# A hand-planned attention and MLP kernel: weight loads that either SyncE or ScalarE may issue, and larger planned costs for SyncE's transfers

## The chip, the cores and the metric

One core of one Trainium2 chip runs the kernel. The metric is the device time of one execution in microseconds, the median of several runs. Matmuls run on TensorE (PE), elementwise work on VectorE (DVE) and ScalarE (ACT), memsets on GpSimd (POOL). Transfers are issued by SyncE (SP) or ScalarE and carried out by 16 DMA engines which all issuers share.

## The reference

Attention in which a query sees only the keys of its own hash bucket, then a two-layer MLP on its output. In numpy, cut to what matters:

```python
# q, k, v: (4, 8, 768, 64) fp32; proj: (64, 6); w_in: (512, 2048); w_out: (2048, 512)
q_bucket = sum(((q @ proj) > 0) * 2**arange(6)); k_bucket likewise
scores = where(q_bucket == k_bucket, q @ k.T / 8, -1e9)
attn = softmax(scores)
x = (attn @ v), heads side by side            # (3072, 512)
h = x @ w_in
g = where(h > 0, h, exp(min(h, 0)) - 1)
out = g @ w_out                               # (3072, 512)
```

## The kernel before

**Numbers.** The values have the precision of fp32, but the matmuls are fast ones on f16: a number is split into a high f16 part and the rest, and three products (high-high, high-rest, rest-high) are summed. So nearly every operand has a "hi" and a "lo" operation.

**Tiles and stages.** The 4 batches are cut in half along the queries: 8 chunks of 384 queries. In each chunk 4 pairs of heads make 32 pairs, n = 0 to 31; each pair has 6 score tiles of 128 queries by 768 keys, 192 in all. A tile goes: scores on PE (L946), maximum on DVE (L969), exponential with sum on ACT (L997), normalised hi (L358) and lo (L363) into a buffer hl, transposed by a DMA of SP into PT (L1053), and the average with v on PE (L1130). PT has two slots of three tiles each. The first four pairs have no hi and lo: PE turns their probabilities (flip, L1013) and the turned tiles are moved out of PSUM into PT by ACT or DVE.

Queries and keys of a pair are loaded by SP, scaled and split, and transposed by a DMA of SP (K at L731, Q at L771; pair 0 on PE). The sign bits come from a small matmul z (L805), a test on DVE (L826, into zb) and small copies of SP (L835) into the transposed operand, two to four for each Q or K. For chunk 0 the loads of its four pairs come first of all.

**Weights.** The 32 slices of w_in and w_out (512 KB each) come in as raw 64-bit words by SP (L464). Every fourth goes to one area of its own ("raw", one slot), the others into U, which has three slots. ACT then takes the top half of each word (L480), DVE joins it with the low one into W (L483) and with that frees the slot; PE squares and sums the slice for a bound on its size (acc, L494). When all of w_in or w_out has been bounded, the slices are split into hi and lo. The MLP of a chunk follows on PE as 16 blocks of F (h, L1192), with E, R, M, H, L on ACT and DVE (L1216 to L363), and of S (o, L1244), interleaved with the scores of the next chunk.

**What sets the order.** Each operation is registered by `add` (L72) with the engines that may run it, its reckoned duration (`took`), a due place, its dependences and ring buffers. `order` (L104) is a list scheduler: again and again it takes the operation that can begin earliest on any engine (the smallest due place decides among those that can begin at once), and its sequence becomes the program order of each engine's queue. An engine other than the first of its list takes an operation only if the first is busy more than YIELD longer (0.9 us before 240 us, 2.5 us after). For SP a transfer lands at `dma + 1000 + slow`: `dma` is a running end of the transfers (each adds its `late`), and `slow` delays the landing alone. A bulk load (weights, v) isn't issued before `dma - BACKLOG` (4.5 us), and at most 8 transfers of SP are under way. The loads of the weights follow each other in order of their number. Where PE would idle in the first 32 us the list puts in dummy matmuls ("spin", L1337).

Durations and landings are only the plan's: on the chip every queue runs its instructions in the planned order, and each waits for its semaphores.

Of the kernel before, what the change touches and what calls it, by code (L numbers as in the profile page):

```python
# [34 lines left out]
NEAR = {"P": 0.0, "V": 0.0, "A": 0.0, "S": 0.0, "G": 0.0}  # L35
BACKLOG = 4500.0
VD = -40
YIELD = (900.0, 2500.0)
FULL = 240e3
STRICT = ("v",)  # L40
# [14 lines left out]

class Op:

    __slots__ = ("engs", "eng", "run", "took", "late", "due", "deps", "after", "new", "left", "next", "start", "free", "end", "slow", "bulk", "cols", "name")

    def __init__(self, **kw):  # L60
        self.start = None
# [5 lines left out]
class Plan:  # L67
# [4 lines left out]
    def add(self, engs, run, took, due, deps=(), after=(), new=(), use=(), late=0.0, slow=0.0, bulk=False, cols=128, name=""):  # L72
        o = Op(
            engs=engs, eng=None, run=run, took=dict(zip(engs, took if type(took) is tuple else (took,))), late=late, due=due, deps=[d for d in deps if d], after=[a for a in after if a],
            new=list(new), slow=slow, bulk=bulk, cols=cols, name=name,
        )
        for b in (*new, *use):
            b.users.append(o)
        self.ops.append(o)
        return o  # L80

    def seen(self, o, e):
        return o.free if o.eng == e and e != "S" else o.end

    def ready(self, o, e):
        t = o.start[e]
# [17 lines left out]
    def order(self):  # L104
        ops = self.ops
        for o in ops:
            o.left = len(o.deps) + len(o.after)
            for d in o.deps:
                d.next.append(o)
            for a in o.after:  # L110
                a.next.append(o)
        open_ = {e: [] for e in "PVAGS"}

        def opened(o):
            o.start = {e: max([0.0] + [self.seen(d, e) for d in o.deps] + [a.start for a in o.after]) for e in o.engs}
            for e in o.engs:
                open_[e].append(o)

        free = {e: 0.0 for e in open_}
        cols = 128  # L120
        dma = 0.0
        sent = []
        for o in ops:
            if o.left == 0:
                opened(o)
        done, spun = [], []
        while len(done) < len(ops):
            best = None
            for e, waiting in open_.items():
                at, some = None, []  # L130
                for o in waiting:
                    t = self.ready(o, e)
                    if t is None:
                        continue
                    t = max(t, free[e])
                    if e == "S" and o.bulk:
                        t = max(t, dma - BACKLOG)
                    if e != o.engs[0] and free[o.engs[0]] < t + YIELD[t > FULL]:
                        continue
                    some.append((t, o.due, o, e))  # L140
                if some:
                    near = min(x[0] for x in some) + NEAR[e]
                    at = min((x for x in some if x[0] <= near), key=lambda x: x[1::-1])
                if at is not None and (best is None or at[0] < best[0]):
                    best = at
            assert best is not None, [(e, [(o.name, o.due) for o in w][:6]) for e, w in open_.items()]
            t, _, o, e = best
            o.eng = e
            for x in o.engs:
                open_[x].remove(o)  # L150
            for b in o.new:
                b.slot = len(b.ring.made) % b.ring.cap
                b.ring.made.append(b)
            took = o.took[e]
            if e == "P":
                if self.spin is not None and t < SPIN[1]:
                    gap = t - max(free[e], SPIN[0]) - SPIN[2]
                    if gap > 0.0:
                        spun.append(self.spin(max(free[e], SPIN[0]), int(gap // 214.0) + 1))
                elif t < COLD:  # L160
                    took *= 1.8
                if o.cols != cols:
                    took += SWITCH
                    cols = o.cols
            if e == "S":
                if len(sent) >= 8:
                    t = max(t, sent[-8])
                dma = max(dma, t + 950.0) + o.late
                o.end = dma + 1000.0 + o.slow
                sent.append(o.end)  # L170
            else:
                o.end = t + took + o.late + SIGNAL[e]
            o.start = t
            o.free = free[e] = t + took
            o.left = None
            done.append(o)
            for x in o.next:
                x.left -= 1
                if x.left == 0:
                    opened(x)  # L180
        return sorted(spun + done, key=lambda o: o.start)
# [18 lines left out]
def lsh_attention_moe(  # L200
# [10 lines left out]
    nc = tc.nc  # L211
    B, H, S, D = q.shape
# [32 lines left out]
    add = plan.add  # L245
# [197 lines left out]
    def weight_ops():  # L443
# [4 lines left out]
        def one(i):  # L448
            o = int(i >= NSI)
# [9 lines left out]
                src = wo64[(i - NSI) * P : (i - NSI + 1) * P, :]  # L459
            due = i - 14.0 + 0.4 * o * (i - NSI)  # L460

            def load():
                t.t = area["raw" if raw else "U"][t.slot]
                nc.sync.dma_start(t.t["in"], src)  # L464

            l = add("S", load, 460.0, due - 6, after=([first_k["q"]] if i == 2 else []) + staged[-1:], new=[t], late=1600.0, slow=1000.0, bulk=True, name=f"w{i}load")
            staged.append(l)
            if not raw:
                in_u.append(i)
# [121 lines left out]
    def prep_ops(ns):  # L591
# [11 lines left out]
        for n, p in zip(ns, ps):  # L603
# [6 lines left out]
            def track(o):  # L610
                regs.append(o)
                return o
# [96 lines left out]
        for x, (n, p) in enumerate(zip(ns, ps)):  # L709
# [9 lines left out]
            if kw:  # L719
                nat, K = buf(f"natk{own}"), buf("K")  # L720
                kbuf[b, p] = K

                def k_hi(e, i=i, s=s, x=x):
                    times(s["natk"][:, :, :D], i["kf"], sc.t[:, x : x + 1], e)

                def k_lo(i=i, s=s, x=x):
                    left_over(s["natk"][:, :, D:], i["kf"], sc.t[:, x : x + 1], s["natk"][:, :, :D])

                def k_tr(K=K, s=s):
                    K.t = [okp.tile([P, 2 * NC, P], F16, tag=y, name=y, bufs=NP) for y in ("K1", "K2")]  # L730
                    nc.sync.dma_start_transpose(K.t[0], flat(s["natk"]))  # L731

                def k_dup(K=K):
                    nc.vector.tensor_copy(flat(K.t[1])[:D], flat(K.t[0])[:D])

                hi = track(add("AV", k_hi, either(2 * NC * D, pointer=True), due - 1, [chain], new=[nat], use=[sc, i["kb"]], name=f"k{n}hi"))
                lo = track(add("V", k_lo, vec(2 * NC * D, 1, True), due - 1, [hi], use=[sc, i["kb"], nat], name=f"k{n}lo"))
                if n == 0:

                    def k_new(K=K):  # L740
                        K.t = [okp.tile([P, 2 * NC, P], F16, tag=y, name=y, bufs=NP) for y in ("K1", "K2")]

                    tr = turned(s["natk"], k_new, lambda K=K: K.t[0], K, nat, [lo], due, f"k{n}tr")
                    first_k["tr"] = tr[-1]
                else:
                    tr = [track(add("S", k_tr, 1700.0, due, [lo], new=[K], use=[nat], late=2100.0, name=f"k{n}tr"))]
                dup = add("V", k_dup, vec(2 * NC * P, 4), due + 3, tr, use=[K], name=f"k{n}dup")
                cps = bits_ops(
                    f"k{n}", [(0, lambda u, K=K: flat(K.t[0])[:, u * HALF : (u + 1) * HALF]), (1, lambda u, K=K: flat(K.t[0])[:, u * HALF : (u + 1) * HALF])],
                    4, 0, lambda u, K=K: flat(K.t[1])[D : D + 2 * NB, u * HALF : (u + 1) * HALF], tr, [K], due + 3, 8, n < DIRECT,  # L750
                )
                kdone[b, p] = [*tr, dup, *cps]
# [23 lines left out]
            if n == 0:  # L776
                tr = turned(s["qq"], q_new, lambda O=O: O.both, O, nat1, [lo, dup], due + 1, f"q{n}tr", (nat2,))
            else:
                tr = [track(add("S", q_tr, 1700.0, due + 1, [lo, dup], new=[O], use=[nat1, nat2], late=2100.0, name=f"q{n}tr"))]
            i["tr"] = tr  # L780
            first_k.setdefault("q", tr[-1])
        both = [ns] if w == 2 else [[n] for n in ns]
# [14 lines left out]
    def bits_ops(name, ways, quads, which, target, deps, use, due, mms, direct):  # L797
# [34 lines left out]
        for u in range(quads):  # L832

            def copy(u=u):
                nc.sync.dma_start(target(u), zb.t[u * QD : u * QD + 2 * NB])  # L835

            cps.append(add("S", copy, 760.0, due, [s], use=[zb, *use], late=100.0, name=name + "cp"))
        return cps


# [76 lines left out]
    def pair_ops(n):  # L917
# [8 lines left out]
        for at in range(2 * HC):  # L926
# [112 lines left out]
            for y, (g, t_, PT_, pt_, _) in enumerate(duo):  # L1039
# [10 lines left out]
                def trp(t_=t_, PT_=PT_, hl=hl, make=make):  # L1050
                    if make:
# [7 lines left out]
                lows[g] = [h]  # L1059
                filled.append(  # L1060
                    add(
                        "S", trp, 1650.0, g + 2.0, [l], after=[] if make else PT_.users[:1], new=[PT_] if make else [],
                        use=[hl] + ([] if make else [PT_]), late=2100.0, name=f"tr{g}",
                    )
                )
        x16, av = buf("x16"), buf("av")
# [307 lines left out]
```

## Time and profile before

| | |
|---|---|
| median of 3 runs | 857.09 us (855.75 to 858.48) |
| profiled execution | 857.44 us |
| its span, first to last instruction | 855.7 us |
| PE busy | 815.4 us, 95% |
| ACT busy | 707.0 us, 83% |
| DVE busy | 678.9 us, 79% |
| SP's DMA queue, share of the 16 engines' span | 72.5% |

How to read it: a busy time counts instructions that compute, and not those that issue transfers or wait. PE's time is modelled at its ends, since matmuls overlap. In the page's slices each digit is one fortieth of the span (21.4 us) in tenths. The granted clock (PEclk) is TensorE's, as a share of 2.4 GHz; 0.50 is 1.2 GHz. In a timeline the bracket behind an instruction is the idle time of its engine before it, with what ended it.

### The profile page before, as it was taken

To read this page: it belongs to the slowest core of one execution; us is meant where nothing else is said; L and a number is where in the kernel's file an instruction comes from. 1 tells how busy PE (TensorE), PEld (TensorE's weight loads), DVE (VectorE), ACT (ScalarE), POOL (GpSimd) and SP (SyncE) were. 2 spreads that over 40 slices of the span, in tenths; PEclk is the share of its full clock that TensorE was granted. 3 is DMA by queue.
4 is the path that set the end of the run, shared out by engine and by line. 5 is a ranking of instruction groups with operands and counts; after the bars stand their busy time and mean duration, and the time that the engine had idled before them with its cause. 6 is when DMAs were issued, how large, how long until landed. Compare 5 with 4: busy or idle time off the path is not lost. (4 is left out here: it accounts for less than half of the span.)

```text
span 855.7 us, 14941 instructions
## 1 busy us (share of the span) xinstructions
PE 815.4 (95%) x5322; PEld 439.8 (51%) x5322; DVE 678.9 (79%) x1511; ACT 707.0 (83%) x1301; POOL 4.8 (1%) x24
## 2 busy tenths in 40 slices
PE   8897888998999999999999999999999999999997
PEld 3365544554554555555555555545455555555553
DVE  5868999999997877988988788889888777773232
ACT  7789999999987889988988789888888778783543
POOL 2000000000000000000000000000000000000000
PEclk9989999999999999999999999999999999999999
DMA  9769667897889589958888888958877768552101
GB/s 298 191 204 293 200 113 130 164 217 122 169 157 178 112 185 209 201 98 154 173 150 131 144 185 191 212 105 151 154 153 141 130 106 155 99 105 38 38 1 38
DMA packets 364330, 128.21 MB, mean 150 GB/s; under 512 B 339112, under 2 KB 357216, under 8 KB 364256
## 3 DMA queue, kind: packets, MB, share of 16 engines
q1 hardware_dynamic: 363952, 127.13, 72.5%
q8 instruction: 42, 0.69, 0.3%
q14 instruction: 32, 0.26, 0.1%
q10 hardware_dynamic: 304, 0.13, 0.1%
HBM read 35.65 MB, written 6.29 MB: 49 GB/s over the span
## 5 line engine op out<-in xcount | busy, mean ns | idle before, releaser
L1192 PE MATMUL h<-X,W 128*128 128x384 f16 x1536 | 312.0, 326 | 4.1 <-ACT U L1220 4.1
L1244 PE MATMUL o<-W,U 128*128 128x512 f16 x1152 | 307.0, 379 | 0.4 <-DVE U L363 0.4
L997 ACT ACTIVATE pt<-pt,nb,sg 128x768 f32<-128x768 f32 x192 | 195.8, 1021 | 41.2 <-DVE nb L986 41.0
L1192 PEld LDWEIGHTS <-W 128*128 128x128 f16 x1536 | 148.3, 97 | 141.8 <-issue 10.3
L969 DVE TENSOR_SCALAR_CACHE_REDUCE pt<-s 128x768 f32<-128x768 f32 x180 | 171.2, 951 | 16.3 <-PE s L946 15.5
L363 DVE SCALAR_TENSOR_TENSOR hl<-pt,r,hl 128x768 f16<-128x768 f32 x168 | 165.2, 1013 | 8.4 <-ACT hl L358 8.3
L1244 PEld LDWEIGHTS <-U 128*128 128x128 f16 x1152 | 110.3, 97 | 101.8 <-issue 2.8
L946 PE MATMUL s<-K,O 128*128 128x384 f16 x720 | 147.8, 327 | 9.8 <-DVE pt L969 9.2
L358 ACT ACTIVATE hl<-pt,r 128x768 f16<-128x768 f32 x168 | 148.8, 928 | 1.0 <-ACT U L358 0.5
L1223 DVE SCALAR_TENSOR_TENSOR U<-U 128x384 f32<-128x384 f32 x128 | 70.9, 554 | 51.2 <-ACT U L1220 50.8
L946 PEld LDWEIGHTS <-O 128*128 128x128 f16 (+1 forms) x768 | 72.9, 98 | 68.5 <-issue 23.3
L1216 ACT ACTIVATE U<-h,ch 128x384 f32<-128x384 f32 x128 | 73.0, 570 | 40.5 <-PE h L1192 39.4
L358 ACT ACTIVATE U<-U,sgg 128x384 f16<-128x384 f32 x128 | 78.1, 610 | 25.6 <-DVE U L1223 25.6
L363 DVE SCALAR_TENSOR_TENSOR U<-U,sgg 128x384 f16<-128x384 f32 x128 | 78.6, 614 | 22.3 <-ACT U L358 19.9
L1130 PE MATMUL av<-PT,vhl 128*64 128x384 f16 x1008 | 90.2, 327 | 6.3 <-DMA PT<-hl 6.3
L1130 PEld LDWEIGHTS <-vhl 128*64 128x64 f16 x1008 | 57.7, 110 | 37.8 <-issue 11.4
L1220 ACT ACTIVATE U<-h,ch 128x384 f32<-128x384 f32 x128 | 72.9, 570 | 0.0
L1035 DVE TENSOR_SCALAR r<-sm 128x2 f32<-128x2 f32 x84 | 13.9, 166 | 30.5 <-ACT pt L997 30.2
L997 ACT ACTIVATION_READ_ACCUMULATOR pt<-pt,nb,sg 128x1 f32 x192 | 36.9, 192 | 0.0
L1013 PE MATMUL flip<-W,pt 128*128 128x128 f32 x144 | 23.6, 287 | 2.4 <-ACT PT L358 1.6
L358 ACT ACTIVATE X<-av 128x384 f16<-128x384 f32 x28 | 13.5, 481 | 13.6 <-PE av L1130 13.4
L363 DVE SCALAR_TENSOR_TENSOR X<-av,X 128x384 f16<-128x384 f32 x28 | 15.5, 554 | 11.3 <-ACT X L358 11.3
(134 smaller groups left out, 581.3 us busy)
## 6 DMA issues: line engine op xcount, KB each, us to landing
U<-in_moe_w_in_dram SPq DMA_DIRECT2D x12, 512.0 KB
vf<-in_v_dram SPq DMA_DIRECT2D x16, 384.0 KB
U<-in_moe_w_out_dram SPq DMA_DIRECT2D x12, 512.0 KB
qst<-in_q_dram SPq DMA_DIRECT2D x30, 192.0 KB
kst<-in_k_dram SPq DMA_DIRECT2D x14, 384.0 KB
out_dram<-W SPq DMA_DIRECT2D x16, 256.0 KB
PT<-hl SPq DMA_TRANSPOSE x168
W<-in_moe_w_in_dram SPq DMA_DIRECT2D x4, 512.0 KB
```

Source lines behind the costliest of these rows:

```text
L358: nc.scalar.activation(o, x, AF.Copy, scale=s)
L363: nc.vector.scalar_tensor_tensor(o, x, s, hi, ALU.mult, ALU.subtract)
L946: nc.tensor.matmul(s.t[:, y, :HALF], O[x][:rows, j * HC + t, :], K[x][:rows, j * NC + y * HC : j * NC + (y + 1) * HC, :].rearrange("p a b ...
L969: nc.vector.tensor_scalar(pt.t.rearrange("p (n e) -> p n e", n=2), s.t[:, :, :HALF], CLAMP, None, ALU.max, ALU.max, accum_out=m.t[:, y : y ...
L997: nc.scalar.activation(pt_.t, pt_.t, AF.Exp, bias=nb.t[:, y : y + 1], scale=sg_of(n), accum_out=sm.t[:, z : z + 1])
L1013: nc.tensor.transpose(hb.t[:, c * P : (c + 1) * P], pt_.t[:, (y * HC + c) * P : (y * HC + c + 1) * P], eye)
L1130: nc.tensor.matmul(av.t[j * D : (j + 1) * D], vs["hl"][p].t[:, j, c, vx, :], PTs[j].t[:, :, px, c, :], start=y == 0, stop=y == 3 * NC - 1,)
L1192: nc.tensor.matmul(h.t, WH[:, g * KT + t, wx, fc * P : (fc + 1) * P], xbuf[NP * ci + t].t[:, xx, :], start=t == 0 and y == 0, stop=t == KT ...
L1216: nc.scalar.activation(e.t, h.t, AF.Exp, scale=c["ch"])
L1220: nc.scalar.activation(hp.t, h.t, AF.Relu, scale=c["ch"])
L1223: nc.vector.scalar_tensor_tensor(e.t, e.t, -1.0, hp.t, ALU.add, ALU.min)
L1244: nc.tensor.matmul(banks[t][:, :DO], g16.t[:, gx, t * P : (t + 1) * P], WH[:, NSI + 1 + f, wx, :], start=f == 0 and y == 0, stop=f == NF - ...
```

## The change

Weight loads may now be issued by ScalarE as well ("SA" in place of "S"; SyncE is still the first choice), with a reckoned 0.50 us on SyncE and 0.62 us on ScalarE, where 0.46 us stood. What the list does for a transfer (landing, backlog, at most 8 under way) now goes by the operation being a transfer (`dma`) and not by its engine. SyncE's other transfers are reckoned longer, and land later by `SLACK`:

| transfer | reckoned on SP before | after | landing later by |
|---|---|---|---|
| transpose of K | 1.70 us | 1.90 in chunk 0, else 1.80 | 1.0 us |
| transpose of Q | 1.70 us | 2.70 in chunk 0, else 2.30 | 1.0 us |
| copy of bits | 0.76 us | 0.82 us | 0.5 us |
| transpose of probabilities | 1.65 us | 1.78 us | 1.5 us |

```diff
+SLACK = (1500.0, 1000.0, 500.0)
...
-            new=list(new), slow=slow, bulk=bulk, cols=cols, name=name,
+            new=list(new), slow=slow, bulk=bulk, dma="S" in engs, cols=cols, name=name,
...
-        return o.free if o.eng == e and e != "S" else o.end
+        return o.free if o.eng == e and not o.dma else o.end
...
-                    if e == "S" and o.bulk:
+                    if o.bulk:
                         t = max(t, dma - BACKLOG)
...
-            if e == "S":
+            if o.dma:
                 if len(sent) >= 8:
...
-            def load():
+            def load(e="S"):
                 t.t = area["raw" if raw else "U"][t.slot]
-                nc.sync.dma_start(t.t["in"], src)
-
-            l = add("S", load, 460.0, due - 6, after=([first_k["q"]] if i == 2 else []) + staged[-1:], new=[t], late=1600.0, slow=1000.0, bulk=True, name=f"w{i}load")
+                (nc.scalar if e == "A" else nc.sync).dma_start(t.t["in"], src)
+
+            l = add("SA", load, (500.0, 620.0), due - 6, after=([first_k["q"]] if i == 2 else []) + staged[-1:], new=[t], late=1600.0, slow=1000.0, bulk=True, name=f"w{i}load")
...
-                    tr = [track(add("S", k_tr, 1700.0, due, [lo], new=[K], use=[nat], late=2100.0, name=f"k{n}tr"))]
+                    tr = [track(add("S", k_tr, 1900.0 if early else 1800.0, due, [lo], new=[K], use=[nat], late=2100.0, slow=SLACK[1], name=f"k{n}tr"))]
...
-                tr = [track(add("S", q_tr, 1700.0, due + 1, [lo, dup], new=[O], use=[nat1, nat2], late=2100.0, name=f"q{n}tr"))]
+                tr = [track(add("S", q_tr, 2700.0 if early else 2300.0, due + 1, [lo, dup], new=[O], use=[nat1, nat2], late=2100.0, slow=SLACK[1], name=f"q{n}tr"))]
...
-            cps.append(add("S", copy, 760.0, due, [s], use=[zb, *use], late=100.0, name=name + "cp"))
+            cps.append(add("S", copy, 820.0, due, [s], use=[zb, *use], late=100.0, slow=SLACK[2], name=name + "cp"))
...
-                        "S", trp, 1650.0, g + 2.0, [l], after=[] if make else PT_.users[:1], new=[PT_] if make else [],
-                        use=[hl] + ([] if make else [PT_]), late=2100.0, name=f"tr{g}",
+                        "S", trp, 1780.0, g + 2.0, [l], after=[] if make else PT_.users[:1], new=[PT_] if make else [],
+                        use=[hl] + ([] if make else [PT_]), late=2100.0, slow=SLACK[0], name=f"tr{g}",
```

## Rows read from the trace of the kernel before

**Rows 1.** The page: busy us, share and instructions; clock and DMA in 40 slices.
```profile
PE 815.4 (95%) x5322; PEld 439.8 (51%) x5322; DVE 678.9 (79%) x1511; ACT 707.0 (83%) x1301; POOL 4.8 (1%) x24
...
PEclk9989999999999999999999999999999999999999
DMA  9769667897889589958888888958877768552101
```
**Rows 2.** Busy time by stage: stretch, length, busy us (instructions) by engine, clock, DMA, GB/s.
```profile
0.00:100.00 100.00, 85.86 (x624) 48.65 (x624) 77.11 (x197) 82.29 (x169) 4.76 (x24) 0.97 0.84 248
100.00:240.00 140.00, 125.45 (x841) 67.58 (x833) 135.33 (x300) 137.14 (x252) 0.00 (x0) 1.00 0.79 152
240.00:780.00 540.00, 533.01 (x3491) 286.83 (x3488) 444.58 (x975) 454.19 (x822) 0.00 (x0) 1.00 0.79 149
```
**Rows 3.** The same view in steps of 4 us: PE, PEld, DVE, ACT, POOL, clock.
```profile
28.00:32.00 4.00, 3.78 (x30) 1.66 (x30) 3.86 (x12) 0.10 (x1) 0.00 (x0) 1.00 0.44 101
32.00:36.00 4.00, 3.84 (x26) 1.98 (x24) 3.93 (x12) 3.14 (x6) 0.00 (x0) 1.00 0.48 92
36.00:40.00 4.00, 2.17 (x20) 1.12 (x18) 2.00 (x5) 2.53 (x8) 0.00 (x0) 1.00 0.99 297
40.00:44.00 4.00, 2.42 (x18) 1.51 (x18) 2.73 (x5) 4.00 (x10) 0.00 (x0) 0.90 0.66 205
44.00:48.00 4.00, 2.76 (x14) 1.92 (x13) 2.58 (x7) 1.31 (x4) 0.00 (x0) 0.50 0.40 77
```
**Rows 4.** Timeline of SP's queue, 22 to 96 us: start, length, instructions.
```profile
22.35 0.53 SPq L464 DMA_DIRECT2D W<-in_moe_w_in_dram  x1
...
28.20 3.22 SPq L835 DMA_DIRECT2D K<-zb  x4
31.52 1.54 SPq L835 DMA_DIRECT2D O<-zb  x2
33.16 1.47 SPq L731 DMA_TRANSPOSE K<-natk  x1
34.68 1.82 SPq L464 DMA_DIRECT2D U<-in_moe_w_in_dram  x3
...
47.97 0.45 SPq L464 DMA_DIRECT2D W<-in_moe_w_in_dram  x1
...
95.09 0.37 SPq L464 DMA_DIRECT2D U<-in_moe_w_out_dram  x1
```
**Rows 5.** Timeline of DVE: the joins of the first three loads into U.
```profile
26.03 1.88 DVE L483 SCALAR_TENSOR_TENSOR W<-U,X 128x512 int32<-128x512 int32 x3
```
**Rows 6.** Timeline of ACT, 32 to 48 us: the instructions behind its longest gaps.
```profile
32.46 1.03 ACT L997 ACTIVATE pt<-pt,nb,sg 128x768 f32<-128x768 f32 x1 [4.36 <-DVE nb L986]
...
39.34 0.78 ACT L480 ACTIVATE X<-U 128x512 f16<-128x512 bf16 x1 [1.47 <-DMA U<-in_moe_w_in_dram]
...
47.01 0.49 ACT L358 ACTIVATE PT<-flip 128x384 f32<-128x384 f32 x1 [2.54 <-PE flip L1013]
```
**Rows 7.** Timeline of PE: the bound sum behind the late decode.
```profile
40.90 0.40 PE L494 MATMUL acc<-W 128*128 128x128 bf16 x4 [2.05 <-DVE W L483]
```
**Rows 8.** Line 401, the issues on ACT's queue: min/median/max ns, first and last start.
```profile
L401 ACTq DMA_DIRECT2D pf<-in_proj_dram x2: 559/586/612, 0.8 to 1.4; - x2
```
**Rows 9.** Line 1053, the transposes of probabilities, in the same form.
```profile
L1053 SPq DMA_TRANSPOSE PT<-hl x168: 1382/1688/3224, 116.4 to 770.6; - x168
```
**Rows 10.** Waits from 240 to 780 us: total us, times, longest.
```profile
PE av L1130 <- DMA PT<-hl: 5.3, 4, 1.7
...
PE z L805 <- DMA O<-natq: 1.0, 1, 1.0
```
**Rows 11.** Waits of SP's queue from 56 to 100 us, in the same form.
```profile
SPq L464 <- DVE W L483: 19.9, 14, 4.5
```

More of the change, by code (lines that the diff above doesn't have):

```diff
@@ L56 @@
 class Op:
-    __slots__ = ("engs", "eng", "run", "took", "late", "due", "deps", "after", "new", "left", "next", "start", "free", "end", "slow", "bulk", "cols", "name")
+    __slots__ = ("engs", "eng", "run", "took", "late", "due", "deps", "after", "new", "left", "next", "start", "free", "end", "slow", "bulk", "dma", "cols", "name")
     def __init__(self, **kw):
```

## The prediction

> **What bounds the kernel now.** I read the page's totals first, then the busy time by stage, then the one stretch where everything stands still, and last the waits of the long middle stage.
>
> The totals [rows 1] show PE busy for 815.4 of 855.7 us, so TensorE is the bound over the whole span, and nothing can win more than its 40 us of gaps plus what a lowered clock costs. The stages [rows 2] tell where these gaps are. From 240 to 780 us PE is busy 533.0 of 540 us: 7.0 us of gaps. From 100 to 240 us PE is busy 125.5 of 140, while ACT has 137.1 and DVE 135.3: there ACT and DVE are the bound. In the first 100 us nobody is: PE 85.9, DVE 77.1, ACT 82.3. This is the stage of the weight loads, and a microsecond won there passes on, since what follows is a stage of work that ACT and DVE must do in any case and then one that PE must do in any case. The tail after 780 us holds none of the edited operations.
>
> Inside the first stage the stretch from 28 to 48 us stands out [rows 3]. Between 36 and 40 us PE, DVE and ACT are all half idle together. The clock then falls: 0.90 for 40 to 44 us and 0.50 for 44 to 48 us, which is 1.2 GHz, the lower of the two levels, just after PE's gaps. And right before, from 28 to 36 us, the DMA engines are at 0.44 and 0.48 with about 100 GB/s, while a moment later they do 297 GB/s at 0.99. The transfers were not short of engines; they had not been issued. The queue of SP shows why [rows 4]: K's four bit copies at 28.20 take 3.22 us (0.80 each), then O's two, then a transpose at 33.16, and only at 34.68 come three weight loads into U. Their three slots had been free since the three joins of DVE that run from 26.03 for 1.88 us, so until 27.91 [rows 5]. These loads stood 6.8 us behind small copies. The chain goes on: ACT's first decode of them starts at 39.34 after waiting for that DMA (4.66 us after issue) [rows 6], and PE's next bound sum at 40.90 waits 2.05 us for the join behind that decode [rows 7].
>
> **The change part by part: the loads.** ScalarE may take a weight load when the list finds SP busy more than 0.9 us longer (2.5 us after 240 us, where no weight load is left). The loads that SP issues directly behind transposes or copies are the candidates: one at 22.35, three at 34.68, four from 47.97 to 52.76, two at 79.40 and 80.01, and the one at 95.09, 11 of 32 [rows 4] (the first, the last and two places between). Copies count 0.82 us in the list and one alone is no ground to move a load, a transpose or a run of them is. I expect 6 to 10 loads on ACT, and take 8.
>
> What it gives: the loads of 34.68 could be issued at about 28.0, where ACT has just begun 4.36 us of idleness, waiting for the scores' bias until 32.46 [rows 6]. With 4.66 us to landing their data is there by 33, so ACT's waits of 1.47 us at 39.34 and, as the clock has no reason to fall, 2.54 us at 47.01 (for flips at the lower clock) go [rows 6]; a few tenths of the same kind follow until 52 us. I put the sum at 4.9 us of ACT. What is late next there is the chain of scores, maximum and bias; it is not touched.
>
> What it costs: an issue on ACT is seen in the two small loads of proj, 0.559 and 0.612 us [rows 8], the only ones behind no other work; for a 512 KB load no row exists on ACT. 0 is the lower bound (in one of ACT's holes), 0.61 the upper one. I take 0.45, between them, nearer to the upper row, and let half of the 8 fall into holes: 4 x 0.45 = 1.8 us. Bounds: 0 to 8 x 0.61 = 4.9 us. SP gets the same instructions off its queue, which is worth nothing by itself: SP waits far longer than it issues. Net of the loads: -4.9 + 1.8 = -3.1 us. The far end is that the whole stretch of 36 to 48 us is repaired: PE's gaps of 1.83, 1.58 and 1.24 us and the clock's 0.10 x 4 + 0.50 x 4 = 2.4 us [rows 3], 7.1 us in all, with free issues.
>
> **The larger costs and later landings.** They execute nothing. They change the order: operations of PE, DVE and ACT that need a transpose or a copy are listed later by 1.5 us (probability transposes), 1.0 us (K and Q) and 0.5 us (bits), and SP's own list is spread wider. The new 1.78 for a probability transpose stands against a median of 1.688 us [rows 9], the old 1.65 was also close, so SP's pace hardly changes. The landing is the part that matters: between 240 and 780 us PE waits 5.3 us in four waits for those transposes (the weight loads' view of PE, PEld, counts the same gaps) and 1.0 us for a Q transpose [rows 10]. Together that is 6.3 of the 7.0 us of gaps. A later listing puts F and S blocks in front of the average, work that is there. A wait vanishes where it is under 1.5 us; four waits of 1.3 us mean are around that. But each later average also holds its PT slot longer (two slots), and the next transposes into it begin later, so part of a wait comes back. I take a third of the 7.0 us: -2.3 us. Bounds: -6.3 us, all of them gone, and +6.3 us, as many new ones of the same size.
>
> **Sum.** The profiled execution is 857.44 us, 855.7 of span and 1.7 around it; the median of the three runs, 857.09, is 0.35 below, which is nothing here. 857.44 - 3.1 - 2.3 = 852.0 us.
>
> **A rule against it.** The DMA engines at 0.44 between 28 and 36 us [rows 3] say that a load issued earlier would land earlier. The Trainium skill (DMA: Bandwidth & Descriptors, section "Issuing engines are not separate DMA queues") holds that issuing from several engines only saves the sequencer's time to initiate a transfer, all of them running on the same 16 engines. By that rule the change would be near nothing, the second rival below; the trace disagrees for this stretch, since what holds the loads is their place behind SP's other instructions, not the engines.
>
> **The rivals.**
> First, faster by far: every gap named is repaired, 857.4 - 7.1 - 6.3 = 844.0 us. For it speaks that both stretches have one plain cause each. Against it, that the orders of five engines shift together, and that from 60 us on loads are limited by free slots, not by SP. Chance 0.10.
>
> Second, no change: the loads come earlier, yet the stage up to 100 us ends when it did. From 56 to 100 us the loads wait for the joins of DVE, 14 times, 19.9 us [rows 11], so SP is not what holds most of them, and the engines have little room: with only the issue time saved, 8 x 0.37 us of an SP [rows 4] that waits anyway, and the waits for PT merely moved, it is 857.4 + 0 to 1.8 us, 857 to 859. Chance 0.25.
>
> Third, slower: a load listed on ACT is not ready when ACT reaches it. Loads wait on a slot which the join on DVE frees, 1.42 us each (19.9 / 14) [rows 11]. On SP nobody stands behind such a wait; on ACT the exponentials, decodes and evictions do, and PE's flips behind these. From 60 to 240 us ACT has nothing to give [rows 2]. Four such waits (5.7 us) undo the 3.1 us and add 2.6 us; six cost 8.5 us, which with no gain from the landings gives 857.4 - 3.1 + 8.5 = 862.8 us. It decides from the fourth on. For it speaks that the list's times and the chip's drift apart; against it, that the candidates stand in stretches where their slots had been free for microseconds (6.8 us for those at 34.68). Chance 0.17.
>
> That the change does not do what it says, no load on ACT at all because copies of 0.82 us never reach 0.9 us, belongs to the second rival in its time; transposes of 1.9 and 2.7 us make it unlikely.
>
> **How the numbers follow.** About 0.3% (2.6 us) is what a measurement of this kernel can tell from no change. The forecast, 852.0, has 0.48; its own range is 848 to 857 (the loads from -4.9 with free issues to 0 with 4.9 of issues, the landings from two thirds of 7.0, -4.6, to 0), and the larger part, 0.42, is below 854.5. With the first rival's 0.10: faster 0.52. Within 0.3%: the second rival's 0.25 and the forecast's upper part, 0.06: 0.31. Slower: 0.17. To leave out no more than 0.2 the range reaches from 845.0, a little above the first rival, to 861.0, short of the third rival's six waits.
>
> **What would show each step.** In the profile after: weight loads on ACT's queue, the first of them near 28 us; the share of the DMA engines in 28 to 36 us above 0.6; no clock of 0.50 near 46 us; ACT's hole before 39 us gone; the granted clock of the first 100 us at 0.99 or more. For the landings: PE's waits for PT between 240 and 780 us under 3 us. Wrong would be the forecast if ACT idles behind its own load issues, waiting for joins (third rival), if the stage of ACT and DVE that follows begins as late as before although the first loads come sooner (second rival), or if new waits of PE for scores or F blocks stand where the PT waits were.

## The result and the profile after

The changed kernel takes 846.23 us (843.60 to 849.16, 4 runs) where the kernel before took 856.78 in the same sitting: a ratio of 0.9876, with a 95% interval of 0.983 to 0.992. It is faster by 10.5 us, about twice the 5.4 that were forecast, and inside the range of 845 to 861. Two of its runs lie near 843.7 us and two near 849, so that the median stands between two groups. The profiled execution is 849.16 us with a span of 847.4, so it is one of the longer ones and stands 8.3 us below the profiled one of before (857.44). What probably sets it apart from the shorter ones, a hole at 84 us, is shown below.

The page of the kernel after, the lines that answer to [rows 1]:

```profile
span 847.4 us, 14946 instructions
...
PE 814.8 (96%) x5322; PEld 439.1 (52%) x5325; DVE 679.3 (80%) x1513; ACT 707.4 (83%) x1299; POOL 4.8 (1%) x24
...
PEclk9999898999999999999999999999999999999999
DMA  8979657987989789987969787968888777551101
```

The work is the same (PE 814.8 us, before 815.4); only gaps can have gone. Where they went is told by the stages, which answer to [rows 2] (stretch, length, busy us of PE, PEld, DVE, ACT, POOL, clock, share of the DMA engines, GB/s):

```profile
0.00:100.00 100.00, 85.19 (x612) 49.85 (x615) 76.27 (x198) 80.52 (x165) 4.76 (x24) 0.97 0.90 249
100.00:240.00 140.00, 127.82 (x827) 67.05 (x829) 135.34 (x300) 137.35 (x251) 0.00 (x0) 0.96 0.76 149
240.00:780.00 540.00, 539.81 (x3558) 290.29 (x3555) 448.38 (x984) 460.51 (x833) 0.00 (x0) 1.00 0.78 150
```

From 240 to 780 us PE's gaps are 540 - 539.81 = 0.2 us instead of 7.0: 6.8 of the 8.3 us. No wait of PE for a transposed probability or a Q is left in that stage. Up to 240 us PE has been busy for 213.0 us instead of 211.3. Busy time also holds the dummy matmuls, and PE's total differs between executions (815.4 us before, 812.4 in e6 below), so a safer measure is the work that PE still has to do at 780 us, here before and after:

```profile
780.00:856.00 76.00, 71.12 (x380) 36.72 (x377) 21.87 (x40) 33.33 (x60) 0.00 (x0) 1.00 0.06 21
```
```profile
780.00:856.00 76.00, 62.01 (x331) 31.92 (x328) 19.30 (x33) 29.02 (x53) 0.00 (x0) 0.99 0.06 21
```

It is 9.1 us less, 6.8 of them won in the long stage, so some 2 us come from before 240 us. Two opposite things are hidden in this small lead. The stretch which the prediction was built on has become better, as the 4 us steps show that answer to [rows 3]:

```profile
28.00:32.00 4.00, 3.94 (x31) 1.94 (x30) 3.97 (x11) 0.85 (x3) 0.00 (x0) 1.00 1.10 279
32.00:36.00 4.00, 3.99 (x33) 2.08 (x30) 3.86 (x14) 2.13 (x4) 0.00 (x0) 1.00 0.99 213
36.00:40.00 4.00, 2.50 (x20) 1.63 (x19) 3.38 (x9) 3.63 (x8) 0.00 (x0) 1.00 0.71 194
40.00:44.00 4.00, 3.11 (x35) 2.17 (x34) 2.31 (x5) 4.00 (x9) 0.00 (x0) 1.00 0.79 184
44.00:48.00 4.00, 3.50 (x29) 2.19 (x28) 3.22 (x7) 2.61 (x7) 0.00 (x0) 1.00 0.45 111
```

The clock stays at 1.00, the DMA engines are busy from 28 us on, and PE does 17.0 us in these 20 instead of 15.0. ACT issues two loads in front of its hole, and the first decodes (from 38.15) wait for no transfer:

```profile
27.71 0.35 ACTq L465 DMA_DIRECT2D U<-in_moe_w_in_dram  x1
...
28.41 0.55 ACTq L465 DMA_DIRECT2D U<-in_moe_w_in_dram  x1
33.21 1.03 ACT L998 ACTIVATE pt<-pt,nb,sg 128x768 f32<-128x768 f32 x1 [4.36 <-DVE nb L987]
...
38.15 0.78 ACT L481 ACTIVATE X<-U 128x512 f16<-128x512 bf16 x1
```

But a new hole has opened at 84 us. The timelines of SP, ACT and PE there, each in its own order:

```profile
76.23 2.60 SPq L772 DMA_TRANSPOSE O<-natq  x1
78.93 0.57 SPq L465 DMA_DIRECT2D U<-in_moe_w_out_dram  x1
```
```profile
76.81 0.36 ACTq L465 DMA_DIRECT2D U<-in_moe_w_out_dram  x1
...
88.51 0.78 ACT L481 ACTIVATE X<-U 128x512 f16<-128x512 bf16 x1 [4.21 <-DMA U<-in_moe_w_out_dram]
```
```profile
89.67 0.90 PE L1014 MATMUL flip<-W,pt 128*128 128x128 f32 x3 [4.76 <-ACT PT L359]
```

SP starts a transpose of Q at 76.23, ACT issues a weight load 0.58 us later, and ACT then waits 4.21 us for a load; by the order of the decodes it is this one, and it lands 11.7 us after its issue (88.51 - 76.81). PE stands behind it for 4.76 us. In steps of 2 us the DMA engines are full and move little:

```profile
80.00:82.00 2.00, 1.56 (x16) 1.13 (x16) 2.00 (x6) 2.00 (x4) 0.00 (x0) 1.00 1.19 101
82.00:84.00 2.00, 1.43 (x11) 0.89 (x9) 1.85 (x4) 2.00 (x5) 0.00 (x0) 1.00 1.27 105
84.00:86.00 2.00, 0.55 (x3) 0.31 (x3) 0.48 (x3) 0.31 (x2) 0.00 (x0) 1.00 1.04 68
86.00:88.00 2.00, 0.00 (x0) 0.00 (x0) 0.00 (x0) 0.00 (x0) 0.00 (x0) 0.55 1.24 140
```

The share is 1.04 to 1.27 at 68 to 140 GB/s, and the clock falls to 0.55 behind the gap (1.2 GHz for most of the step). In all, ScalarE took five loads: four from 27.7 to 36.5 us and this one.

So three questions stood: is the steady gain due to the landings, the larger durations or the loads; what are the four early loads worth; what does the late one cost?

### The profile page after: what moved, and what is told of

It is laid out like the page before. It is cut to its first block, busy times and chain, and to the rows that moved or that the text cites. A ratio compares the mean times of both kernels' runs of the same rounds, so it can differ in the third digit from the quotient of the medians.

```text
span 847.4 us, 14946 instructions
## 1 busy us (share of the span) xinstructions
PE 814.8 (96%) x5322; PEld 439.1 (52%) x5325; DVE 679.3 (80%) x1513; ACT 707.4 (83%) x1299; POOL 4.8 (1%) x24
## 4 chain that ended last, share of the span: by engine, by line
PE 64%; DVE 1%; ACT 1%; issue 0%; ACTq 0%
PE o L1245 23%; PE h L1193 23%; PE s L947 9%; PE av L1131 8%; PE z L806 1%; DVE hl L364 0%; DVE pt L970 0%; ACT U L1217 0%; ACT U L1221 0%; ACT pt L998 0%; DVE U L364 0%; DVE U L1224 0%; ACT U L359 0%; ACT hl L359 0%; ACT po L1279 0%
## 5 line engine op out<-in xcount | busy, mean ns | idle before, releaser
L1193 PEld LDWEIGHTS <-W 128*128 128x128 f16 x1536 | 148.1, 97 | 139.5 <-issue 10.2
L364 DVE SCALAR_TENSOR_TENSOR U<-U,sgg 128x384 f16<-128x384 f32 x128 | 78.6, 614 | 21.3 <-ACT U L359 18.4
L1131 PE MATMUL av<-PT,vhl 128*64 128x384 f16 x1008 | 87.2, 327 | 0.0
L1131 PEld LDWEIGHTS <-vhl 128*64 128x64 f16 x1008 | 54.7, 110 | 32.2 <-issue 8.3
L1338 PE MATMUL spin<-ones 128*128 128x512 bf16 x81 | 22.9, 415 | 2.6 <-POOL ones L370 2.4
L987 DVE TENSOR_SCALAR nb<-m,sg 128x2 f32<-128x2 f32 x96 | 21.9, 228 | 3.0
```

The costliest lines, as they stand in the source:

```text
L364: nc.vector.scalar_tensor_tensor(o, x, s, hi, ALU.mult, ALU.subtract)
L1131: nc.tensor.matmul(av.t[j * D : (j + 1) * D], vs["hl"][p].t[:, j, c, vx, :], PTs[j].t[:, :, px, c, :], start=y == 0, stop=y == 3 * NC - 1,)
L1193: nc.tensor.matmul(h.t, WH[:, g * KT + t, wx, fc * P : (fc + 1) * P], xbuf[NP * ci + t].t[:, xx, :], start=t == 0 and y == 0, stop=t == KT ...
L1338: nc.tensor.matmul(x, ones, ones[:, :1].to_broadcast([P, 512]), start=True, stop=True)
```

## The experiments

Theory A is that the later landings give the gain from 240 to 780 us by the order of PE's work. Rival B gives it to the loads, rival C to the larger durations alone. Theory S says that the late load on ScalarE's queue, beside SyncE's transpose, makes the hole at 84 us.

**The parts one by one.** The first four kernels ran on one chip beside the kernel before (858.59 us).

e1, the loads alone:

```diff
-SLACK = (1500.0, 1000.0, 500.0)
+SLACK = (0.0, 0.0, 0.0)
# and 1900/1800, 2700/2300, 820, 1780 back to 1700, 1700, 760, 1650
```

> Only the weight loads may go to ScalarE (0.50 and 0.62 us reckoned); the landing delays are zero and the transposes and copies are reckoned as before. Theory A (the later landings make the gain, by the order of PE's work between 240 and 780 us): PE's gaps from 240 to 780 us stay near the 7.0 us of before (5 to 9), and the time is 853 to 858, the early stage giving 0 to 4 us. Rival B (the loads make the gain): the time is 846 to 850, with PE's gaps in 240 to 780 us under 2 us.

Measured: 861.58 us, ratio 1.0045 (1.0015 to 1.0075). In its stage from 240 to 780 us the gaps are 8.1 us:

```profile
240.00:780.00 540.00, 531.86 (x3499) 288.20 (x3500) 446.16 (x978) 457.32 (x827) 0.00 (x0) 1.00 0.80 150
```

ScalarE issued three loads at 27.4 to 29 us, as wished, and yet the kernel is not faster, rather 0.45% slower. Theory A had the gaps right and the time wrong (853 to 858); B falls.

e2, the landing delays alone (loads on SyncE, all durations as before):

```diff
-            l = add("SA", load, (500.0, 620.0), due - 6, ...
+            l = add("S", load, 460.0, due - 6, ...
# and the four durations back to those of before
```

> Only the landing delays of 1.5, 1.0 and 0.5 us; all loads stay on SyncE and every reckoned duration is that of before. Theory A: PE's gaps from 240 to 780 us fall from 7.0 to under 2 us, PE's waits for PT vanish, and the time is 848 to 852 with the early stage as before. Rival B: gaps of 5 to 9 us remain and the time is 854 to 860.

Measured: 849.81 us, ratio 0.9914 (0.9886 to 0.9943), and the gaps are 2.0 us:

```profile
240.00:780.00 540.00, 537.96 (x3550) 289.18 (x3549) 447.26 (x984) 457.17 (x827) 0.00 (x0) 1.00 0.78 149
```

PE's waits for PT are gone, as expected by theory A; what is left are 1.8 us of scores that wait for DVE.

e3, the larger durations alone:

```diff
-SLACK = (1500.0, 1000.0, 500.0)
+SLACK = (0.0, 0.0, 0.0)
# and the loads add("S", load, 460.0, ...) as before
```

> Only the larger reckoned durations of SyncE's transposes and copies; no landing delay, loads on SyncE with 0.46 us as before. Rival C (the truer pace of SyncE's queue makes the gain): PE's gaps from 240 to 780 us fall under 3 us, time 849 to 853. Theory A: gaps 4 to 9 us, time 854 to 860.

Measured: 853.15 us, ratio 0.9951 (0.9936 to 0.9966), gaps 3.8 us:

```profile
240.00:780.00 540.00, 536.18 (x3540) 289.21 (x3537) 448.55 (x987) 458.23 (x829) 0.00 (x0) 1.00 0.80 151
```

Neither theory had this quite: the gaps lie a little under theory A's 4 to 9 us, the time just under its 854 to 860. In that stage the durations alone take 3.2 us off the gaps, where the landings alone took 5.0. Its early stage holds a result against the prediction: the three loads that stood at 34.68 before come still later here,

```profile
46.33 1.45 SPq L465 DMA_DIRECT2D U<-in_moe_w_in_dram  x3
```

and yet the granted clock is 1.00 in all steps from 28 to 48 us, PE does 16.9 us of work in them instead of 15.0, and the kernel is faster. ACT and PE are given scores and flips there, which need no load.

e4, the changed kernel again, for the hole at 84 us:

> The changed kernel once more, for the stretch from 84 to 89 us, where the profiled execution stands still for 4.2 us behind a weight load that came late. If the stall belongs to this order of transfers (theory S), it is there again with 3 to 5 us; if it is an accident of that execution (rival), ACT's wait for that load is under 1 us, and the span is about 4 us shorter, near 843.

Measured: 848.39 us, ratio 0.9904 (0.9876 to 0.9932). The hole is there again, with a wait of 2.75 us for the load, a little under the 3 to 5 expected; ScalarE had issued the late one at 77.50, SP its transpose at 76.65. So it is no accident of one execution.

**Parts taken out of the changed kernel.** These four ran on another chip (before: 858.80 us).

e5, only the first 12 loads may go to ScalarE:

```diff
-            l = add("SA", load, (500.0, 620.0), ...
+            l = add("SA" if i < 12 else "S", load, (500.0, 620.0) if i < 12 else 500.0, ...
```

> The changed kernel, but only the first 12 weight loads may go to ScalarE; in the plan this takes one load off ScalarE's queue, the 27th, which it issued at 76.8 us beside a running transpose of Q. Theory S (a load on the second queue beside SyncE's transpose slows both): the stretch of 4 to 8 us at about 100 GB/s between 80 and 88 us shrinks to 2 us, ACT's wait of 2.7 to 4.2 us for that load falls under 1.5 us, and the time is 2 to 5 us below that of the changed kernel, 843 to 847. Rival (the order of decodes behind the transpose makes the stall): the wait stays at 2.5 us or more, time 847 to 850.

Measured: 842.02 us (840.61 to 848.86), ratio 0.9809 (0.9762 to 0.9855). The hole at 84 us is gone: ACT waits 0.40 us for a load there, and no step of 2 us from 76 to 94 us moves less than 203 GB/s. Its profiled execution, however, is the longest of its four (848.86; the others 840.61 to 842.11), with a hole of the same kind elsewhere. ScalarE's early loads, at 27.50 and 28.20, enclose a transpose of K which SP starts at 27.94, and what waits is this transpose. Waits of the first 100 us, engine and line, what they waited for, us in total, times, longest:

```profile
ACT PT L359 <- DMA K<-natk: 7.2, 1, 7.2
...
DVE K L735 <- DMA K<-natk: 6.1, 1, 6.1
```

e6, no load on ScalarE, all else as changed:

```diff
-            l = add("SA", load, (500.0, 620.0), ...
+            l = add("S", load, 500.0, ...
```

> The changed kernel with all weight loads on SyncE (0.50 us reckoned): landing delays and larger durations without the move. If the loads on ScalarE are worth 3 us in the early stage, as the prediction's sum says, this is 3 us or more above the changed kernel, 850 to 854. If they are worth nothing or cost something, it is the same or less, 844 to 849.

Measured: 843.54 us (842.84 to 845.32), ratio 0.9814 (0.9786 to 0.9842). The landings and durations without any move of loads give all of the gain and more. Its stages show where:

```profile
0.00:100.00 100.00, 86.55 (x645) 49.01 (x646) 80.86 (x204) 86.73 (x180) 4.76 (x24) 1.00 0.83 249
100.00:240.00 140.00, 129.75 (x852) 68.03 (x850) 135.74 (x301) 136.84 (x250) 0.00 (x0) 0.98 0.79 154
240.00:780.00 540.00, 539.65 (x3534) 290.14 (x3533) 444.26 (x977) 458.81 (x829) 0.00 (x0) 1.00 0.79 150
```

Up to 240 us PE has been busy for 216.3 us, 5.0 more than before, and at 780 us it has 56.5 us of work left where 71.1 were left before:

```profile
780.00:880.00 100.00, 56.47 (x300) 29.00 (x298) 17.73 (x31) 25.55 (x46) 0.00 (x0) 0.98 0.03 10
```

Of these 14.6 us the long stage gives 6.6, so some 8 us come from before 240 us. The order alone repairs the early stage too, and not by an earlier place of the loads. The three loads that the prediction wanted to move stand where they stood, at 34.54 us (34.68 before), and the DMA engines are idle in front of them, at 0.14:

```profile
34.54 1.45 SPq L465 DMA_DIRECT2D U<-in_moe_w_in_dram  x3
```
```profile
32.00:36.00 4.00, 3.99 (x32) 2.19 (x26) 3.96 (x11) 3.67 (x8) 0.00 (x0) 1.00 0.14 23
```
```profile
39.37 0.77 ACT L481 ACTIVATE X<-U 128x512 f16<-128x512 bf16 x1
```

What has changed is the order on ACT: it runs exponentials and moves turned tiles from 32.33 us on and comes to its first decode of these loads at 39.37 without a wait. (e6 also reckons the loads at 0.50 us on SP instead of 0.46; what that alone does was not run.)

e7, the changed kernel with SLACK at zero:

```diff
-SLACK = (1500.0, 1000.0, 500.0)
+SLACK = (0.0, 0.0, 0.0)
```

> The changed kernel with the three landing delays at zero: loads on both queues and larger durations. Theory A (order by landings): PE's gaps from 240 to 780 us come back to 3 to 5 us, as with the larger durations alone, time 852 to 856. Rival: the two other parts make most of the gain and the time stays within 2 us of the changed kernel, 846 to 850.

Measured: 855.39 us, ratio 0.9959 (0.9936 to 0.9982), gaps from 240 to 780 us 540 - 536.74 = 3.3 us: theory A. Its late load on ScalarE is another one, at 77.42, 0.58 us behind SP's transpose at 76.84, and here again it is the transpose that is late: ACT waits 5.8 us for it.

e8, the delays doubled:

```diff
-SLACK = (1500.0, 1000.0, 500.0)
+SLACK = (3000.0, 2000.0, 1000.0)
```

> The changed kernel with the landing delays doubled to 3.0, 2.0 and 1.0 us. If a later listing costs nothing once the waits are gone, PE's gaps from 240 to 780 us stay under 1 us and the time is within 2 us of the changed kernel. If the slots held longer give waits back, as the prediction feared, the gaps rise by 2 us or more and the time is 850 or above.

Measured: 880.06 us, ratio 1.0242 (1.0207 to 1.0278). The second case, and far beyond it: gaps of 19.8 us from 240 to 780 us. Most of them are not for transfers any more, but between the engines; PE's longest sum of waits there:

```profile
240.00:780.00 540.00, 520.21 (x3400) 277.33 (x3398) 439.99 (x967) 447.95 (x808) 0.00 (x0) 1.00 0.77 148
```
```profile
PE s L947 <- DVE pt L970: 13.4, 11, 2.5
```

PE waits for the bank of the scores, which the maximum on DVE frees late. That the slots of PT, held longer, cause this was expected but not shown; it could as well be another buffer behind the maximum. Nor do these gaps make the whole loss of 21.3 us: they are 12.8 us more than before. Another part is a hole from 35 to 46 us like that of e5. ScalarE issues two loads from 27.53 us on, SP a transpose of K at 27.80, and DVE waits for this transpose, with PE behind it; waits of the first 240 us:

```profile
PE z L806 <- DVE zb L827: 11.5, 2, 11.3
...
DVE K L735 <- DMA K<-natk: 8.1, 1, 8.1
```

**The move of the loads by itself.** The last four kernels keep every queue's order as in the changed kernel and change, behind the plan, only which engine issues certain loads. They ran on one chip, before at 857.71 us, and make a table of two by two.

e9 is the changed kernel itself:

> The changed kernel, as the reference of the three that follow: five loads on ScalarE, four near 27 to 36 us and one near 77 us. By what two executions showed, 843 to 849, with ACT's wait of 2.7 to 4.2 us between 84 and 89 us.

e10 puts the late load onto SyncE's queue, at its place in the order:

```diff
     ops = plan.order()
+    for o in ops:
+        if o.name == "w26load":
+            o.eng = "S"
```

> Every queue in the order of the changed kernel; only the load near 77 us is issued by SyncE, behind the transpose of Q instead of beside it. Theory S (a load on ScalarE's queue beside SyncE's transpose slows both): no stretch of more than 2 us under 150 GB/s between 80 and 88 us, ACT's wait there under 1.5 us, time 2 to 5 us below the changed kernel. Rival (the load's earlier place is worth more than it disturbs): the load lands later, ACT's wait grows beyond 4 us and the time is the same or above.

e11 does so with the four early ones ("w5load" to "w8load"):

> Every queue in the order of the changed kernel; only the four early loads are issued by SyncE, between its copies. Theory of the prediction: their data come later, ACT waits 1.5 us or more for them near 38 us and the time is 2 to 4 us above the changed kernel. Theory S alone: the time is the same or up to 2 us below, since K's transpose at 29 us has no second queue beside it.

e12 does both:

> Both moves back, all loads on SyncE in the order of the changed kernel. If the two moves act apart from each other, the difference to the changed kernel is the sum of the two single ones: by theory S 842 to 845, by the prediction's theory of early loads 848 to 852.

| median us (ratio to before, 95%) | late load on ScalarE | late load on SyncE |
|---|---|---|
| early four on ScalarE | e9: 847.49 (0.9839 to 0.9913) | e10: 842.31 (0.9795 to 0.9860) |
| early four on SyncE | e11: 848.27 (0.9856 to 0.9919) | e12: 843.25 (0.9801 to 0.9866) |

Down each column the early four on ScalarE give 0.8 and 0.9 us, within the runs' spread. Along each row the late load on ScalarE costs 5.2 and 5.0 us. Theory S foretold the cost of the late load; the prediction's 2 to 4 us for the early loads do not hold. The hole is in the profile of e11 (a wait of 4.31 us at 89.79 behind a load issued 0.81 us after the transpose) and not in those of e10 and e12. In e10 the transpose starts at 78.53 us and SP issues the load behind it, at 80.74:

```profile
78.53 2.11 SPq L772 DMA_TRANSPOSE O<-natq  x1
80.74 1.04 SPq L465 DMA_DIRECT2D U<-in_moe_w_out_dram  x2
```

In the stretch behind it e10 reads:

```profile
80.00:82.00 2.00, 1.89 (x20) 1.45 (x19) 2.00 (x5) 1.91 (x4) 0.00 (x0) 1.00 1.27 267
82.00:84.00 2.00, 1.33 (x11) 0.72 (x10) 2.00 (x6) 1.86 (x4) 0.00 (x0) 1.00 0.97 245
84.00:86.00 2.00, 1.75 (x15) 1.20 (x15) 2.00 (x5) 2.00 (x6) 0.00 (x0) 1.00 1.07 426
86.00:88.00 2.00, 1.35 (x9) 0.81 (x9) 1.48 (x6) 2.00 (x5) 0.00 (x0) 1.00 1.00 395
```

Where the changed kernel moved 68 to 140 GB/s, this one moves 245 to 426, and ACT decodes the load at 87.10 without a wait. The move changes two things at once: the queue, and the distance behind the start of the transpose (2.21 us instead of 0.58). Which of them counts is not separated. The profiled execution of e9 has no hole and is the shortest of its six (841.55 us; the others 846.78 to 849.89); that the others have one is inferred from their times. Of all 14 executions of the changed kernel three lie below 844 us and eleven above 846.5. In the profiled one of e9 the late load follows the transpose of Q by 1.60 us (74.46 and 76.06):

```profile
74.46 2.50 SPq L772 DMA_TRANSPOSE O<-natq  x1
```
```profile
76.06 0.33 ACTq L465 DMA_DIRECT2D U<-in_moe_w_out_dram  x1
```

In the four profiles with the hole at this place it follows by 0.58 (the kernel after), 0.85 (e4), 0.81 (e11) and 0.58 us (e7). That the distance decides is a guess from five executions, and nearness alone is not enough: a load of e10 at 36.30 us, 0.31 us behind a transpose, left no wait for a transfer above 1.8 us from 34 to 50 us. e10, which is the changed kernel with one load moved back, is faster than both kernels, and so are e5, e6 and e12 by their ratios to before (0.9809 to 0.9834, the changed kernel 0.9876 to 0.9904); between these four no order can be told.

## Why the prediction was right, and where it was not

**The bound.** The stages were read rightly: PE's gaps were all there was to win, 7.0 us of them from 240 to 780 us [rows 2], and they did go.

**The landings.** The mechanism was right and the size was not: -2.3 us were put down, a third of the gaps. Alone (e2) they took 5.0 us off the gaps of the long stage (7.0 to 2.0) and 8.8 us off the time; with the larger durations the gaps went to 0.2 us. The fear behind the third, that a PT slot held longer gives waits back, is no term at 1.5 us: no wait of PE for a transfer is left. At 3.0 us it may be one, but e8 does not show it: its gaps of 19.8 us are mostly waits for the maximum. So a landing reckoned later is worth much up to some value and costs beyond it; no row of before shows where that is, and between 1.5 and 3.0 us nothing was run.

**The larger durations.** They were costed at nothing, since 1.78 us differs little from 1.65 beside a median of 1.688 [rows 9]. This step failed. Alone they took 3.2 us off PE's gaps in the long stage and 5.4 us off the time (e3: 853.15 against 858.59), and together with the landings, all loads on SyncE, the gain is 15.3 us (e6) where the landings alone gave 8.8 (e2, on another chip). The prediction compared the reckoned and the real time for the transposes of PT only; the Q transposes of the first 100 us, reckoned at 1.7 us, took 1.45 to 3.74 us before. Which of the durations makes the gain was not tested.

**The loads.** -3.1 us were put down, -4.9 of holes and +1.8 of issues. This step failed too. The holes went as described: no decode waits near 39 us, the clock stays up [rows 3, 6]. But the move is not what closed them. e12 has the early loads on SyncE, between its copies from 30.80 us on, and is only 0.9 us above e10, which has them on ScalarE; e1, with three loads moved and the old order, gains nothing; e6 leaves the three loads at 34.54 and e3 puts them at 46.33, and both are faster than before. Moving the four loads is worth 0.8 to 0.9 us by the table, within the spread, and not 3.1. The prediction read rightly that the loads came late, and took their lateness for the cause, where in e3 and e6 it was enough that ACT had other work listed in front of their decodes. ACT's hole of 4.36 us [rows 6] stood unchanged, as it waits for the bias. It expected 8 loads on ScalarE; there were 5. The issues themselves took 0.33 to 0.55 us each, close to the 0.45 that was put down [rows 8].

**The rivals.** The second rival, loads that come earlier and change nothing, is near the truth for the four early loads. The third, slower by loads on ScalarE, came true in part by another mechanism: no issue of ACT stood waiting for a slot; instead one load ran beside a transpose of SP, and cost 5 us. For the same reason one of the prediction's own signs failed: the granted clock of the first 100 us was to be 0.99 or more and is 0.97, by the fall behind the hole at 84 us. The first rival's time, 844.0, is what the kernels without the late load reach and pass (842.0 to 843.5).

**Right in the mechanism of one term, and by luck in the time.** The terms -2.3 and -3.1 do not stand for what happened. By the table the order of the changed kernel with all loads on SyncE is worth -14.5 us (e12, 843.25 against 857.71), the four early loads -0.9 and the late one +5.2: together -10.2, as measured for e9. The order was undervalued by far, and the late load, which the prediction did not foresee, took a third of its gain away. Without it the time would be near 842 us (e10), below the range of 845 to 861: the unforeseen loss keeps the result inside.

**The rule.** The prediction weighed a rule of the Trainium skill (DMA: Bandwidth & Descriptors, section "Issuing engines are not separate DMA queues") and held that the trace disagreed: engines at 0.44 while loads stood behind copies. For the four early loads the table of two by two agrees with the rule, 0.8 and 0.9 us. The row was right and the conclusion was not: in e6 the engines still stand at 0.14 there, and the kernel is faster all the same.

## What to carry to other kernels

When loads stand behind small transfers in one queue, first look whether the engine that waits for them has other work that could be listed in front: here the order gave what the second queue was meant to give, with the loads as late as before (e6), and moving four of them was worth under 1 us. Before a load goes to a second queue, look for transposes of the first queue that run at that moment; one load beside one cost 5 us in the median. In a list-scheduled kernel a reckoned landing that is too early was paid here on the busiest engine (7.0 us of gaps), and one that is too late was paid too (19.8 us): try it on both sides.

## What the runs showed of the hardware

In the kernel after, a plain load of 512 KB on ScalarE's queue, issued 0.58 us behind the start of a DMA transpose of SyncE's queue, came with a stretch of some 8 us in which the 16 DMA engines were full (1.04 to 1.27) at 68 to 140 GB/s, and landed 11.7 us after its issue. In the four profiles with this hole (0.58 to 0.85 us behind) ACT waited 2.75 to 5.8 us for the load or the transpose; e5 and e8 show a like hole where loads of ScalarE enclose a transpose of K (waits of 7.2 and 8.1 us). The same load on SyncE's queue, 2.21 us behind the same transpose, did not (245 to 426 GB/s), nor did it on ScalarE's queue 1.60 us behind (e9). Why the two queues disturb each other, and whether the queue or the distance decides, is open.
